# Memory rows copied into v's own tile, sums by four-column products, router inputs turned by PE, and reordered units, in a kernel of chunked attention and top-2 experts

## The chip, the cores and the metric

The kernel runs on one core of a Trainium2 chip. A core has five engines with lists of their own: PE (TensorE, matrix products; its weight loads are shown as PEld), DVE (VectorE), ACT (ScalarE), POOL (GpSimd) and SP (SyncE, which here only issues DMAs). Sixteen DMA engines serve the DMAs of all of them. Each engine works through its list in order, and waits between engines go over semaphores. The metric is the device time of one execution in microseconds (us); lower is better.

## What is computed

Attention over chunks of 32 queries, each with a context of 16 keys to the left, the chunk itself, 8 to the right, and 8 memory keys of its head; then a router that takes the best two of eight experts for each of the 3072 rows.

```python
for c in range(nc):                                   # 24 chunks of 32
    k_full = np.concatenate([mem_k, k[:, :, l_start:r_end]], axis=2)
    v_full = np.concatenate([mem_v, v[:, :, l_start:r_end]], axis=2)
    scores = scale * np.matmul(q_c, k_full.transpose(0, 1, 3, 2))
    a = np.exp(scores - np.max(scores, axis=-1, keepdims=True))
    a = a / (np.sum(a, axis=-1, keepdims=True) + 1e-09)
    out[:, :, c_start:c_end] = np.matmul(a, v_full)
...
logits = x @ w_gate
noisy_logits = logits + np.log1p(np.exp(x @ w_noise)) * noise
top2 = np.argpartition(-noisy_logits, 2, axis=1)[:, :2]
# the softmax of the two gives the weights of relu(x @ w1[e]) @ w2[e]
```

Shapes: q, k and v are 4 x 8 x 768 x 64 in float32 (batch, heads, rows, depth), mem_k and mem_v 4 x 8 x 8 x 64, x is 3072 x 512, there are 8 experts of 512 x 1024 and 1024 x 512.

## The kernel before

**Units and groups.** The attention is cut into 16 units (NPAIR). A group g of four heads has two units, each with half of the 24 chunks. q and k of a group are loaded by POOL into qg and kg (three buffers each), v into one of three tiles vg (load_v, four DMAs, L120). In a tile vg each head has 32 partitions: 28 hold the context rows (two rows side by side), the last four are for memory and are zero in this kernel. For that, each of the three tiles is cleared once, in pieces, by DVE (zero_v, L136), ACT (clear_v, L159) and POOL (L570, L571).

**A unit's steps**, in the main loop from L576. Iteration i works at several units at once: PT_pe(i-1) turns the probabilities on PE, max_dve(i) takes the maximum of the scores (L298), qkT_pe turns q and k of a later head pair (L250), PT_dve(i-1) copies the turned probabilities to SBUF (L317), sub_dve(i) subtracts the maximum on DVE (sd, L303) and takes the exponential on ACT (P, L305). kT_act copies the turned keys in two halves on ACT (kd, L261), PV_pe(i-1) makes the value products, scores_pe(i+1) the next scores, mult_dve(i-1) divides by the sum (rec, L342, and xrow, L343), and xT_pe(i-2) turns the rows for the router (p_x, L354; copied to xt, L356). ps_s and ps_o, the PSUM tiles of scores and values, have one buffer, the turned tiles share a ring of three (tag "tr").

**Keys ahead.** ahead(i) says which head pairs are turned in iteration i: i+2 up to iteration 4, both i+2 and i+3 in iteration 5 (NEAR), and i+3 from then on. The scores of an even unit need the keys of two pairs, its own and the next.

**The memory rows.** mem_v is loaded by SP into mv_nat, cast by POOL (memory_values, L186) into a tile memv with one block of columns a head and four more columns of ones. For each of the three blocks u of a unit, two products with memv of 260 columns (L326) start the accumulation: 256 columns of memory values and four of sums over all keys. The products with vg (L330) add the context's values.

**The router.** The weights (wgn_f) and the noise (nz_all) are loaded by SP in rows of 32 bytes (load_router, load_noise), cast on DVE (L227). begin_route(b), after the units of batch b, makes the logits on PE (L365), and the steps of route(b) are run piece by piece in later iterations by early_steps and late_steps, partly on DVE, ACT and POOL. write_rows (L533) writes the rows x and their gates to DRAM from SP's list. After the loop come the last unit, the last batch's routing, the lists of rows for each pair of experts, and the experts: gathers by POOL (L682), products L746 and L754, and scattered writes (L762).

**What sets the order.** The engines' lists are in the order in which the code is written (the schedule is manual); nothing moves an instruction past another of its engine.

Of the kernel before, what the change touches and what calls it, by code (L numbers as in the profile page):

```python
# [12 lines left out]
F32 = mybir.dt.float32  # L13
# [11 lines left out]
def kernel(  # L25
# [59 lines left out]
    def body():  # L85
# [28 lines left out]
        def load_v(g):  # L114
            vg = groups[g][2]
            for hd in range(2 * GP):
# [6 lines left out]

                first, last = gh == 0, gh == B * H - 1
# [12 lines left out]

        new_group(0)
# [8 lines left out]
        mv_nat = ap_.tile([128, NG, 2, D], F32, name="mv_nat", bufs=1)  # L147
        nc.vector.memset(mv_nat, 0.0)
        for hd in range(2 * GP):
            nc.sync.dma_start(  # L150
                out=mv_nat[QW * hd + WP:QW * hd + QW].rearrange("p g e d -> p g (e d)"),
                in_=bass.AP(mem_v.tensor, mem_v.offset + hd * n_mem * D, [[2 * D, n_mem // 2], [2 * GP * n_mem * D, NG], [1, 2 * D]]))
# [11 lines left out]
        for x in range(3):  # L164
            zero_v(0, x)
        load_v(0)
# [10 lines left out]
        memv = ap_.tile([128, NG, 2, OW], BF16, name="memv", bufs=1)  # L177
        nc.vector.memset(memv, 0.0)
        for hd in range(2 * GP):
            p0 = QW * hd  # L180
            nc.vector.memset(memv[p0:p0 + QW, :, :, MD + hd:MD + hd + 1], 1.0)

        def memory_values(lo, hi):
            for hd in range(2 * GP):
                p0 = QW * hd
                nc.gpsimd.tensor_copy(memv[p0:p0 + QW, lo:hi, :, hd * D:hd * D + D], mv_nat[p0:p0 + QW, lo:hi])  # L186

# [3 lines left out]
        wgn_f = rp.tile([128, KP, 2, E], F32, name="wgn_f")  # L191

        def load_router():
            for x, src in enumerate((moe_w_gate, moe_w_noise)):
                nc.sync.dma_start(out=wgn_f[:, :, x, :], in_=src.rearrange("(kp p) e -> p kp e", p=128))
            load_noise(0)

        nz_all = rp.tile([128, NP, E], F32, name="nz_all")

        def load_noise(b):  # L200
            nc.sync.dma_start(out=nz_all[:, b * BT:(b + 1) * BT, :], in_=moe_noise[b * S:(b + 1) * S].rearrange("(t p) e -> p t e", p=128))

# [20 lines left out]
        def constants():  # L223
# [3 lines left out]
            nc.vector.tensor_copy(wgn, wgn_f.rearrange("p k t e -> p k (t e)"))  # L227
# [5 lines left out]
        def memory_keys():  # L233
# [3 lines left out]
            for hh in range(2):  # L237
                nc.scalar.copy(mkd[64 * hh:64 * hh + 64, :, hh, :], p_m[64 * hh:64 * hh + 64])

# [17 lines left out]
        def kT_act(n):  # L257
# [280 lines left out]
        def begin_route(b):  # L538
# [7 lines left out]
            for x in ((1,), (2, 3))[b] if b < 2 else ():  # L546
                load_noise(x)
# [420 lines left out]
```

## Time and profile before

| | us |
|---|---|
| median of 3 runs | 343.18 |
| lowest and highest of them | 341.76, 344.17 |
| the profiled execution, its own time | 340.9 |
| its span in the trace | 339.2 |
| busy in the span: PE, DVE, ACT, POOL | 295.1, 170.8, 132.5, 137.9 |

Attention and routing take about the first 108 us: the first gather is issued at 107.45 us and the first expert product starts at 112.89 us. In the page's slices each digit is the busy share of one fortieth of the span in tenths; PEclk is the clock granted to PE, DMA the mean busy share of the sixteen DMA engines. A row of a view gives the start and length in us, the line and engine, what is written and read, and in brackets the idle time of the engine ahead of it and what ended it. In a row of groups the numbers behind the first bar are the busy time in all and the mean length in ns; behind the second the idle time ahead of the group.

### The profile page before, as it was taken

What the parts mean: (1) busy time and instruction counts of PE and PEld (TensorE: products, weight loads), DVE (VectorE), ACT (ScalarE), POOL (GpSimd) and SP (SyncE); (2) the same over time, 40 slices, a digit from 0 to 9 for tenths busy, and PEclk for the clock granted to TensorE, in tenths of its full rate; (3) what the DMA queues carried; (4) which work ended last, traced back from release to release, by engine and by line L of the source; (5) the groups of instructions that cost most, each with busy time, mean ns of one, the idle gap of its engine ahead of it and who ended that gap; (6) DMA issues with size and microseconds to landing.
All of it is one profiled execution on the core that took longest, in us unless ns stands there. A gap on an engine that the chain in (4) does not pass through costs nothing.

```text
span 339.2 us, 8160 instructions
## 1 busy us (share of the span) xinstructions
PE 295.1 (87%) x3492; PEld 180.0 (53%) x3492; DVE 170.8 (50%) x341; ACT 132.5 (39%) x232; POOL 137.9 (41%) x181
## 2 busy tenths in 40 slices
PE   1687888898753859999999999999999999999990
PEld 1566676776542645548547545545545545545540
DVE  7788779889686653224224233224413424434430
ACT  7867888795430423343333323223123113103100
POOL 8878885392233686400062043034250132141161
PEclk9999999999985699999999999999999999999997
DMA  7999999999991379970059129518849227221031
GB/s 102 183 180 192 187 164 198 221 104 164 228 276 26 96 111 226 224 130 2 2 84 229 31 60 198 95 56 148 181 107 200 57 80 126 40 93 53 6 130 66
DMA packets 58407, 42.87 MB, mean 126 GB/s; under 512 B 32215, under 2 KB 51799, under 8 KB 58368
## 3 DMA queue, kind: packets, MB, share of 16 engines
q0 software_dynamic: 49808, 38.80, 68.9%
q1 hardware_dynamic: 8272, 3.44, 4.7%
q8 instruction: 29, 0.48, 0.5%
q10 hardware_dynamic: 288, 0.07, 0.1%
q14 instruction: 10, 0.08, 0.1%
HBM read 61.32 MB, written 10.65 MB: 212 GB/s over the span
## 4 chain that ended last, share of the span: by engine, by line
PE 54%; issue 16%; DVE 15%; ACT 6%; POOL 5%; DMA 1%; POOLq 0%; DVEq 0%
PE ps_h L746 23%; PE ps_y L754 19%; POOL out_dram L762 4%; ACT kd L261 3%; DVE vg L136 2%; DVE mx L298 2%; DVE sd L303 2%; PE p_t L691 2%; DVE xrow L343 2%; PE ps_o L330 2%; PE ps_o L326 2%; ACT xt L356 2%; ACT P L305 1%; ACT qT L253 1%; PE ps_s L285 1%
## 5 line engine op out<-in xcount | busy, mean ns | idle before, releaser
L746 PE MATMUL ps_h<-xTb,w1t 128*128 128x512 bf16 (+3 forms) x608 | 106.6, 325 | 2.0 <-DVE xTb L692 2.0
L754 PE MATMUL ps_y<-w2t,ht 128*128 128x512 bf16 x448 | 102.0, 379 | 0.0
L746 PEld LDWEIGHTS <-w1t 128*128 128x128 bf16 x864 | 64.1, 97 | 45.2 <-DVE xTb L692 1.6
L762 POOL DMA_INDIRECT out_dram<-acc,sidx x28 | 27.9, 995 | 139.2 <-DVE acc L761 135.0
L734 DVE TENSOR_SCALAR ht<-ps_h 128x416 bf16<-128x416 f32 (+2 forms) x64 | 39.9, 625 | 72.8 <-PE ps_h L746 72.8
L732 ACT ACTIVATE ht<-ps_h 128x416 bf16<-128x416 f32 (+2 forms) x72 | 37.9, 526 | 76.7 <-PE ps_h L746 72.4
L754 PEld LDWEIGHTS <-ht 128*128 128x128 bf16 x448 | 41.9, 98 | 46.6
L758 ACT ACTIVATE acc<-ps_y,meta 128x512 f32<-128x512 f32 x28 | 19.2, 687 | 69.3 <-PE ps_y L754 56.5
L746 PE MATMUL ps_h<-xTs,w1t 128*128 128x32 bf16 x256 | 45.4, 177 | 0.2 <-DVE xTs L707 0.2
L761 DVE SCALAR_TENSOR_TENSOR acc<-ps_y,meta,acc 128x512 f32<-128x512 f32 x28 | 21.0, 751 | 37.0 <-PE ps_y L754 37.0
L682 POOL DMA_INDIRECT xl<-x_rows,gidx x28 | 29.7, 1061 | 15.4 <-issue 6.1
L120 POOL DMA_DIRECT2D vg<-in_v_dram x34 | 25.3, 753 | 8.2 <-PE ps_s L290 3.4
L692 DVE COPY xTb<-p_t 128x512 bf16<-128x512 bf16 x28 | 11.7, 422 | 29.0 <-PE p_t L691 29.0
L261 ACT COPY kd<-p_t 64x768 bf16<-64x768 bf16 x32 | 25.2, 786 | 1.0 <-PE p_t L250 0.7
L250 PE MATMUL p_t<-identb,qg 128*64 128x128 bf16 x192 | 10.3, 245 | 8.2 <-DMA qg<-in_q_dram 6.3
L305 ACT ACTIVATE P<-sd 128x768 bf16<-128x768 f32 x16 | 13.5, 844 | 9.5 <-DVE sd L303 9.5
L356 ACT COPY xt<-p_x 128x768 bf16<-128x768 bf16 x16 | 12.8, 798 | 8.0 <-PE p_x L354 7.7
L343 DVE TENSOR_TENSOR xrow<-ps_o,rec 128x768 bf16<-128x768 f32 x16 | 15.3, 958 | 0.6
L326 PE MATMUL ps_o<-memv,PT 128*128 128x260 bf16 x96 | 13.7, 279 | 2.0 <-DVE PT L317 2.0
L298 DVE TENSOR_REDUCE mx<-ps_s 128x12 f32<-128x768 f32 x16 | 15.1, 941 | 0.6 <-PE ps_s L285 0.6
L303 DVE TENSOR_TENSOR sd<-ps_s,mx 128x768 f32<-128x768 f32 x16 | 15.2, 947 | 0.0
L253 ACT COPY qT<-p_t 128x768 bf16<-128x768 bf16 x16 | 12.8, 800 | 5.0 <-PE p_t L250 4.7
(146 smaller groups left out, 305.6 us busy)
## 6 DMA issues: line engine op xcount, KB each, us to landing
w1t<-in_moe_w_dram POOLq DMA_DIRECT2D x8, 1024.0 KB
w2t<-in_moe_w_dram POOLq DMA_DIRECT2D x8, 1024.0 KB
vg<-in_v_dram POOLq DMA_DIRECT2D x30, 168.0 KB
qg<-in_q_dram POOLq DMA_DIRECT2D x7, 384.0 KB
kg<-in_k_dram POOLq DMA_DIRECT2D x7, 384.0 KB
x_rows<-xrow SPq DMA_DIRECT2D x3, 792.0 KB
x_rows<-xrow SPq DMA_DIRECT2D x2, 384.0 KB
xl<-x_rows,gidx POOLq DMA_INDIRECT x28
```

The source lines that it names most:

```text
L120: nc.gpsimd.dma_start(out=vg[p0 + j:p0 + j + nj, c:c + n, hd, :, :].rearrange("p c e d -> p c (e d)"), in_=bass.AP(v.tensor, v.offset + (g ...
L261: nc.scalar.copy(st[n]["kT"][hs, hh, :].rearrange("d (p j) -> d p j", j=SJ), st[n]["p_k"][hs].rearrange("d j p -> d p j"))
L298: nc.vector.tensor_reduce(out=mx, in_=st[n]["ps"], axis=AX, op=Alu.max)
L303: nc.vector.tensor_tensor(out=sd, in0=st[n]["ps"], in1=bc4(st[n]["mx"], CTX), op=Alu.subtract)
L343: nc.vector.tensor_tensor(out=xr.rearrange("p u (h d) -> p u h d", d=D), in0=po[:, :, :MD].rearrange("p u (h d) -> p u h d", d=D), in1=rec ...
L682: nc.gpsimd.indirect_dma_start(out=xl, out_offset=None, in_=xd, in_offset=bass.IndirectOffsetOnAxis(ap=gidx[:, p:p + 1], axis=0), bounds_c ...
L732: nc.scalar.activation(out=dst, in_=src, func=Act.Relu)
L734: nc.vector.tensor_scalar(out=dst, in0=src, scalar1=0.0, scalar2=None, op0=Alu.max)
L746: nc.tensor.matmul(out=ps_h[:, o:o + w], lhsT=w1t[:, kp, f * 128:(f + 1) * 128], rhs=rhs(kp), start=(kp == 0 and i == 0), stop=(kp == KP - ...
L754: nc.tensor.matmul(out=ps_y, lhsT=ht[:, f, j * CAP:(j + 1) * CAP], rhs=w2t[:, f, :], start=(f == 0), stop=(f == FB - 1))
L761: nc.vector.scalar_tensor_tensor(out=a, in0=ps_y, scalar=gate, in1=a, op0=Alu.mult, op1=Alu.add)
L762: nc.gpsimd.indirect_dma_start(out=out_part[p], out_offset=bass.IndirectOffsetOnAxis(ap=sidx[:, p:p + 1], axis=0), in_=a, in_offset=None, ...
```

## The change

The memory rows go into the four spare partitions of each head in vg. POOL loads them once, cast to bfloat16, into a small tile mv of 16 partitions, and load_v has, ahead of each head's v load, one more DMA on SP's list: it copies four partitions of mv into vg, the same row for each of the 24 chunks. memv, mv_nat, memory_values and their clearing go. The 260-column products become products with headb, a constant of four columns (one a head), which give only the sums; the products with vg give the memory's values with the others.

Pieces of the second and third vg tile that DVE and POOL cleared are now cleared by POOL as 32-bit words (wipe_v).

The noise and the router weights are loaded at the start as rows of 4 KB into 32 partitions (rowsT), three DMAs on SP. After unit 3, router_turn turns them with eight products on PE and copies them into nz_all and wgn with three copies on ACT. The later noise loads and the cast go.

The units' order: ahead(i) is always i+2. From unit 1 on the first half of the key copies goes ahead of the exponential on ACT, the second stays behind it. begin_route goes behind the value products and the next scores. In the last iteration late_steps comes ahead of the value products, and mult of unit 14 goes behind PT of unit 15; xT of unit 14 goes behind the last value products.

```diff
+                nc.sync.dma_start(out=vg[p0 + WP:p0 + QW, :, hd, :, :].rearrange("p c e d -> p c (e d)"),
+                                  in_=mv[MP * hd:MP * hd + MP, g:g + 1, :].to_broadcast([MP, ncnk, 2 * D]))
...
+        def wipe_v(x, lo, hi):
+            nc.gpsimd.memset(vbufs[x][:, lo:hi].bitcast(I32), 0)
+
+        NW = 2 * KP
+        rowsT = ap_.tile([NP + NW, 128, E], F32, name="rowsT", bufs=1)
+        nc.sync.dma_start(out=rowsT[:NP], in_=moe_noise.rearrange("(t p) e -> t p e", p=128))
+        for x, src in enumerate((moe_w_gate, moe_w_noise)):
+            nc.sync.dma_start(out=rowsT[NP + KP * x:NP + KP * (x + 1)], in_=src.rearrange("(kp p) e -> kp p e", p=128))
...
-        mv_nat = ap_.tile([128, NG, 2, D], F32, name="mv_nat", bufs=1)
-        nc.vector.memset(mv_nat, 0.0)
...
+        MP = QW - WP
+        mv = ap_.tile([2 * GP * MP, NG, 2 * D], BF16, name="mv", bufs=1)
...
+        nc.gpsimd.dma_start(out=mv, in_=bass.AP(mem_v.tensor, mem_v.offset, [[2 * D, 2 * GP * MP], [2 * GP * n_mem * D, NG], [1, 2 * D]]))
         load_v(0)
...
-        memv = ap_.tile([128, NG, 2, OW], BF16, name="memv", bufs=1)
-        nc.vector.memset(memv, 0.0)
+        headb = const.tile([128, 2 * GP], BF16, name="headb")
+        nc.vector.memset(headb, 0.0)
         for hd in range(2 * GP):
...
+            nc.vector.memset(headb[QW * hd:QW * hd + QW, hd:hd + 1], 1.0)
...
+        def router_turn():
+            p_n = psT.tile([128, E, NP + NW], F32, name="p_n", tag="tr")
+            for e in range(E):
+                nc.tensor.transpose(out=p_n[:, e, :], in_=rowsT[:, :, e], identity=ident)
+            nc.scalar.copy(nz_all, p_n[:, :, :NP].rearrange("p e t -> p t e"))
+            for x in range(2):
+                nc.scalar.copy(wgn[:, :, E * x:E * x + E], p_n[:, :, NP + KP * x:NP + KP * (x + 1)].rearrange("p e k -> p k e"))
...
-        def kT_act(n):
+        def kT_act(n, which=(0, 1)):
...
-                    nc.tensor.matmul(out=po[:, u, :OW], lhsT=PT[:, 2 * u + e, :], rhs=memv[:, g, e, :], start=(e == 0), stop=False, skip_group_check=True)
+                    nc.tensor.matmul(out=po[:, u, MD:OW], lhsT=PT[:, 2 * u + e, :], rhs=headb, start=(e == 0), stop=(e == 1), skip_group_check=True)
...
-        memory_values(0, 2)
-        nc.gpsimd.memset(vbufs[1][:, 12:15], 0.0)
-        nc.gpsimd.memset(vbufs[1][:, 21:24], 0.0)
+        wipe_v(1, 12, 15)
+        wipe_v(1, 21, 24)
+        wipe_v(1, 6, 12)
         def ahead(i):
-            return [i + 2] if i < NEAR else [n for n in (i + 2, i + 3) if n < NPAIR and (i == NEAR or n > i + 2)]
+            return [i + 2] if i + 2 < NPAIR else []
...
-            if fresh:
-                begin_route((i - 3) // HP)
             early_steps()
             if i >= 1:
                 PT_dve(i - 1)
+            if i >= 1:
+                for n in ahead(i):
+                    kT_act(n, (0,))
             sub_dve(i)
             if i == 0:
-                zero_v(1, 1)
                 load_v(1)
...
+            if i == NPAIR - 1:
+                late_steps()
             for n in ahead(i):
-                kT_act(n)
+                kT_act(n, (1,) if i >= 1 else (0, 1))
...
                 scores_pe(i + 1)
+            if fresh:
+                begin_route((i - 3) // HP)
             if i < NPAIR - 1:
                 late_steps()
-            if i in (2, 3, 4):
-                zero_v(2, i - 2)
-            if i >= 1:
+            if 1 <= i < NPAIR - 1:
                 mult_dve(i - 1)
...
+            if i == 1:
+                wipe_v(2, 0, 12)
...
             if i == 3:
-                zero_v(2, 3, nc.gpsimd)
+                wipe_v(2, 12, 24)
                 ramps()
-                load_router()
+                router_turn()
...
         PT_pe(n)
         PT_dve(n)
-        xT_pe(n - 1)
-        late_steps()
+        mult_dve(n - 1)
+        write_rows(B, B - 1, 0, UB, 0, XC)
         PV_pe(n)
         mult_dve(n)
         write_rows(B + 1, B - 1, UB, BT, 0, XC)
+        xT_pe(n - 1)
         early_steps()
         xT_pe(n)
```

26 lines of the change are left out of this document (1 added, 25 removed).

## The prediction

> **What bounds the kernel now.** I read the slices of the page first, then the chain that ended last, then the rows of each engine in order of time, then the DMA view by windows.
>
> ```profile
> PE   1687888898753859999999999999999999999990
> ...
> PEclk9999999999985699999999999999999999999997
> DMA  7999999999991379970059129518849227221031
> ```
>
> A slice is 8.5 us. From slice 15 on PE is full and DMA often idle: the expert products, which the change doesn't touch, set the time there. What the change can move lies in slices 0 to 12, attention and routing, where PE is at 7 to 8 tenths and, what is easily passed over, **DMA at nine tenths or more in every slice from 1 to 11**. The chain of waits goes there from engine to engine:
>
> ```profile
> 13.38 1.34 DVE vg L136
> 14.72 0.82 DVE mx L298
> ...
> 31.29 0.68 ACT kd L261
> 31.99 0.80 ACT kd L261
> 33.40 0.96 DVE mx L298
> ```
>
> So three things are late by turns: memsets on DVE (units 0 to 4), key copies on ACT (odd units), and later DVE's own list, with gaps in which DVE waits for PE:
>
> ```profile
> L342 DVE RECIPROCAL rec<-ps_o 128x12 f32<-128x12 f32 x11 | 2.5, 229 | 6.3 <-PE ps_o L330 6.1
> ```
>
> This row is of the window 46 to 98 us: 6.1 us of waiting for the value products before the reciprocal.
>
> **Part 1, the four-column sums.** One unit's PE rows (start, length):
>
> ```profile
> 35.13 0.84 PE L326 MATMUL ps_o<-memv,PT 128*128 128x260 bf16 x6
> 35.91 0.85 PE L330 MATMUL ps_o<-vg,PT 128*32 128x256 bf16 x24
> 36.69 0.31 PE L275 MATMUL ps_s<-mkd,qT 128*128 128x16 bf16 x6
> 36.92 0.51 PE L285 MATMUL ps_s<-kd,qT 128*32 128x112 bf16 x23
> ```
>
> From start to start the six 260-column products take 0.78 us. Six products of 16 columns with the same full weight load (L275) take 0.23; four columns can't be dearer, and the weight load stays. So 0.55 us a unit, 8.8 over 16, of which only that part counts where DVE waits for the value products.
>
> **Part 2, work taken from DVE and POOL.**
>
> ```profile
> L136 DVE MEMSET vg<- 128x1536 uint32 x8 | 10.7, 1338 | 2.3 <-issue 2.3
> ```
>
> Four of the eight L136 memsets leave DVE (5.4 us), and with them the clearing of memv and mv_nat; five far smaller ones come for headb. On POOL the wipes write 32-bit words, 9,216 a partition (2 x 768, 1536, 2 x 3072); at the rate of the row below, 0.87 ns an element, that is 8.0 us. They replace this memset, two of half its size (5.3 us together) and eight casts, so POOL has about as much to do as now, and one more DMA to issue (mv). Its loads are issued well ahead of their turn on the engines (part 5), which hides this; without that cover a load would come up to 8.0 us later.
>
> ```profile
> 34.68 2.66 POOL L136 MEMSET vg<- 128x3072 bf16 x1
> ```
>
> **Part 3, reordering.** Odd units' scores wait for the keys of unit i+2 behind the exponential (the two kd rows above). With one half moved ahead of it, one half, 0.8 us, goes. At unit 5 the before kernel turns two units at once:
>
> ```profile
> 41.63 3.21 ACT L261 COPY kd<-p_t 64x768 bf16<-64x768 bf16 x4
> ```
>
> Half of this, 1.6 us, goes. The price: from unit 7 on odd units wait again for their own keys, which the before kernel had a unit ahead. begin_route goes behind the value products and the scores, so its 24 products no longer stand before them at units 6, 10 and 14:
>
> ```profile
> 85.20 0.74 PE ps_l L365 x24
> ```
>
> **Part 4, router_turn** adds eight 32-bit transposes and three ACT copies after unit 3. Four such took 0.63 us:
>
> ```profile
> 8.63 0.63 PE L236 MATMUL p_m<-ident,mk_nat 32*128 32x32 f32 x4
> ```
>
> So 1.3 us of PE; its PSUM buffer also holds up the next key transposes. I count 1.3 on the path, nothing if PE waits for v then anyway.
>
> **Part 5, the copies on SP.** Per group four DMAs of 4 x 24 rows of 256 bytes, 384 packets; 32 DMAs in all. SP is in order: behind a copy that waits for a buffer stand later copies and the x_rows writes. The waits are for the same value products that POOL's v loads wait for already, and the writes are not needed before the gathers, so I give that nothing; if a write were held up, it would have until the gathers. But the packets use engines that are full:
>
> ```profile
> DMA packets 3315, 0.90 MB, mean 180 GB/s; under 512 B 3009, under 2 KB 3314, under 8 KB 3314
> ...
> DMA packets 879, 0.60 MB, mean 200 GB/s; under 512 B 165, under 2 KB 878, under 8 KB 878
> ...
> DMA packets 3598, 0.83 MB, mean 166 GB/s; under 512 B 3596, under 2 KB 3596, under 8 KB 3596
> ...
> DMA packets 4960, 1.11 MB, mean 186 GB/s; under 512 B 4193, under 2 KB 4960, under 8 KB 4960
> ...
> q1 hardware_dynamic: 2016, 0.06, 43.2%
> ```
>
> These are the windows 34 to 39, 39 to 42, 44 to 49 and 10 to 16 us. Small packets are v, larger ones q and k. In 34 to 39 some 3,009 small ones pass, about a group of v (28 x 24 x 4 = 2,688), then q and k follow: so group 2's v is there at about 39.0. Its user, and the maximum of unit 6 behind it:
>
> ```profile
> 42.28 0.85 PE L330 MATMUL ps_o<-vg,PT 128*32 128x256 bf16 x24
> ...
> 44.76 0.94 DVE L298 TENSOR_REDUCE mx<-ps_s 128x12 f32<-128x768 f32 x1
> ```
>
> Only 3.3 us of slack. The loads run back to back, so a faster attention stage can't have them earlier. By then the copies of groups 0 to 4, 5 x 384 = 1,920 packets, are mixed in. Spread over all engines at v's own rate (3,596 packets in 5 us) they cost 2.7 us; at that of the 2,016 packets of 32 bytes, which left the total at 186 GB/s, nothing. I take 1.3: v of group 2 at 40.3. [...]
>
> **The sum.** First stretch, to the maximum of unit 6: without v the engines gain 0.5 (an estimate between nothing and the 1.34 of the memset that ends at 14.72, when unit 0's maximum starts), 2 x 0.8 (units 1, 3), 2 x 0.55 (units 2, 4), 1.6 (unit 5), and lose 1.3: 3.5, maximum at 41.3. With v at 40.3 and the 2.48 us from L330 to the maximum it comes at 42.8: **-2.0** (ends -3.3 and -0.6). Second stretch, units 6 to 15: of the 6.1 us of waits four are long; 4 x 0.55, and 0.7 at three of them for the routing products, is 4.3. But the transposes of unit i+2 stay ahead of the value products and wait for ACT, and odd units wait for keys (partly covered by DVE's routing steps): **-1.8** (ends -4.3, all of it, and +1, none of it and a quarter us more at each of units 7, 9, 11 and 13). Tail:
>
> ```profile
> 93.75 0.51 PE p_x L354 x6
> ```
>
> xT of unit 14 leaves PE's list before the last value products, the routing steps fill DVE's wait before, and mult of unit 14 goes behind PT of 15: **-0.5** (ends -1, twice the transposes, and +0.5, PT of 15 ahead of that mult and nothing gained). Sum -4.3 us. The profiled execution took 340.9 us, of which 339.2 are the span; it would come to 334.9 and 336.6. The median of the runs shown is 343.18, 2.3 above it, so I predict 338.9.
>
> **The rivals.** Two maxima of DVE, of units 8 and 15, and the sizes of the loads:
>
> ```profile
> 54.81 0.95 DVE L298 TENSOR_REDUCE mx<-ps_s 128x12 f32<-128x768 f32 x1
> ...
> 88.62 0.95 DVE L298 TENSOR_REDUCE mx<-ps_s 128x12 f32<-128x768 f32 x1
> ...
> vg<-in_v_dram POOLq DMA_DIRECT2D x30, 168.0 KB
> qg<-in_q_dram POOLq DMA_DIRECT2D x7, 384.0 KB
> ```
>
> *Slower: the copies pile on a few DMA engines.* A copy writes four partitions. If it runs on four of the 16 engines, always the same, these get 1,920 / 4 = 480 packets more by the time of group 3's v. At v's price, 16 x 5 us / 3,596 = 22 ns on one engine, that is 10.7 us. Behind group 2's v at 39.0 come the 768 KB of q and k of a group and the 672 KB of group 3's v, 3.9 and 4.1 us at the 200 and 166 GB/s of the rows: 47.0, and in this case 57.7. The maximum of unit 8 comes some 2.5 us after the product that uses it, as for unit 6 above: 60.2 in place of 54.8. The seven units from there take 33.8 now and 32.0 with the gain of the second stretch; the tail gains its 0.5. So 343.18 + (60.2 + 32.0 - 88.6) - 0.5 = 346.3. From some 16 ns a packet on it is slower than before. For it: DMA at nine tenths, and no slack to take up a delay; against it: the 32-byte packets that cost nothing, and that v's packets read 512 bytes from DRAM for their 256 and a copy reads half of that from SBUF. [...] No view of this profile names an engine.
>
> *Little change: half of that price.* At 11 ns the 480 packets are 5.3 us: unit 8's maximum at 47.0 + 5.3 + 2.5 = 54.8, where it is now, so that all of the first stretch is lost; and if the odd units' key waits take 0.6 of the later gain, 343.18 + (54.8 + 32.6 - 88.6) - 0.5 = 341.5. For it: bytes in place of packets set the price; against: as above.
>
> *More: the copies are free*, and the waits for the value products go nearly whole: -3.3, -3.5 and -0.7, which is 335.7. For it: the 32-byte packets; against: the transposes and keys that still stand in the same lists.
>
> **How the numbers follow.** Forecast 0.45, free copies 0.13, little change 0.25, slower 0.17. About 1% (3.4 us) is what a measurement of this kernel tells from no change. Faster by more: 0.37 of the forecast and all of the free case, 0.50. Slower by more than 1%, 346.6 and up: the piling case above v's price, or with PE waits that it adds elsewhere, 0.12. Within: 0.38. The range goes from a little below the free case to the piling one, 335 to 347, and leaves out what goes beyond either.
>
> **What would show it.** Right: L326 at about 0.23 us for six; no L136 memset on DVE after 14 us; unit 6's maximum at 42 to 43.5 and unit 15's at 84 to 86; PE waiting before the value products of unit 4 for v. Piling: v loads of one group that land far apart, unit 8's maximum after 56. Wrong would be a maximum of unit 6 as late as now, a wait on the copies themselves in units 0 to 2, or a start of the expert products that moves by another amount than unit 15's maximum.

## The result, and the profile after

The changed kernel takes 359.36 us, the median of four runs (358.79 to 359.57), against 342.75 us for the kernel before on the same chip: 1.051 times as long (95% interval 1.047 to 1.055), some 17 us more. The forecast was 338.9, in a range of 335 to 347. The profiled execution has a span of 357.9 us. A few executions were slower at a lower mean clock (one of e5's four took 352.16 us at 0.950, the other three 345.56 to 348.48 at 0.958 to 0.968); the times and ratios below leave those out.

The page's slices come first; a slice is now 8.9 us. The last line is that of the kernel before, for comparison.

```profile
PE   2718858578776358899999999999999999999990
...
PEclk9976788698888559999999999999999999999997
DMA  7999998999999424998006904913949624421031
GB/s 109 172 167 160 162 131 88 145 209 103 184 192 206 149 80 74 214 192 202 2 3 99 222 4 91 217 27 93 204 114 161 116 97 76 70 99 51 3 126 63
...
GB/s 102 183 180 192 187 164 198 221 104 164 228 276 26 96 111 226 224 130 2 2 84 229 31 60 198 95 56 148 181 107 200 57 80 126 40 93 53 6 130 66
```

The full stretch of PE begins two slices later than before. In slice 2 (counted from 0) PE stands nearly still, its clock is below full in most slices up to 14, and the DMA engines, at eight or nine tenths as before, move less: 131 and 88 GB/s in slices 5 and 6, where it was 164 and 198. The chain of waits says what holds the attention up (start, length, what):

```profile
15.30 0.82 SPq L124
...
17.52 10.46 DMA vg<-mv
...
28.23 1.48 PE ps_o L327 x24
...
32.84 0.24 PE ps_o L323 x6
33.07 0.82 PE ps_o L327 x24
...
36.44 15.87 DMA vg<-in_v_dram
52.30 0.28 issue
52.58 17.42 DMA vg<-in_v_dram
70.01 0.28 issue
70.29 0.75 POOL vg L120
71.06 0.53 POOL oh L427
...
76.01 16.46 DMA vg<-in_v_dram
```

First the copies of the memory rows themselves: issued on SP from 15.3 us, the last of group 0 lands 10.5 us after its issue. Then three v loads of 16 to 17 us each. Before, this part of the chain went from engine to engine. POOL now often issues a load only when an earlier one has landed, 12.3 us of waits by the page's group below (first row; the second is the kernel before), and its routing step oh (L427 in the chain) stands behind these issues.

```profile
L120 POOL DMA_DIRECT2D vg<-in_v_dram x34 | 25.4, 752 | 26.8 <-DMA vg<-in_v_dram 12.3
...
L120 POOL DMA_DIRECT2D vg<-in_v_dram x34 | 25.3, 753 | 8.2 <-PE ps_s L290 3.4
```

DVE's rows show the first of the stalls and the maxima that answer to those of the prediction (units 2, 6, 8 and 15):

```profile
29.77 0.23 DVE L339 RECIPROCAL rec<-ps_o 128x12 f32<-128x12 f32 x1 [9.77 <-PE ps_o L327]
30.04 0.96 DVE L340 TENSOR_TENSOR xrow<-ps_o,rec 128x768 bf16<-128x768 f32 x1
30.91 0.95 DVE L295 TENSOR_REDUCE mx<-ps_s 128x12 f32<-128x768 f32 x1
...
54.68 0.95 DVE L295 TENSOR_REDUCE mx<-ps_s 128x12 f32<-128x768 f32 x1
...
68.31 0.95 DVE L295 TENSOR_REDUCE mx<-ps_s 128x12 f32<-128x768 f32 x1
...
107.03 0.94 DVE L295 TENSOR_REDUCE mx<-ps_s 128x12 f32<-128x768 f32 x1
```

Unit 6's maximum is 9.9 us later than before, unit 8's 13.5, unit 15's 18.4; the first expert product starts at 131.68, 18.8 later. So all of the loss lies ahead of the experts. Three rows of the lists of waits name the cause of the first stall, and what it holds up (what waited, for what, us in total, times, longest). SP can't issue the first copies before 15.3 us, since mv's own load has to land; PE then waits 9.0 us for the copies; and POOL waits 6.9 us for the value products that free a tile, so that the v loads of group 2 are issued from 34.18 us on, where it was 26.68 before:

```profile
SPq L124 <- DMA mv<-in_mem_v_dram: 13.3, 1, 13.3
...
PE ps_o L327 <- DMA vg<-mv: 9.0, 1, 9.0
...
POOL vg L120 <- PE ps_o L327: 6.9, 1, 6.9
```

The windows of 10 us show the clock beside the stall (engines' busy times, then the granted clock, DMA share and GB/s; the second pair is the kernel before):

```profile
10.00:20.00 10.00, 7.23 (x140) 5.82 (x140) 6.16 (x8) 8.76 (x12) 6.42 (x8) 1.00 1.81 168
20.00:30.00 10.00, 1.77 (x32) 1.29 (x33) 0.23 (x1) 1.38 (x2) 7.25 (x8) 0.62 1.78 170
...
10.00:20.00 10.00, 7.15 (x138) 5.88 (x136) 8.70 (x14) 8.49 (x12) 7.59 (x11) 1.00 1.71 189
20.00:30.00 10.00, 8.43 (x198) 6.44 (x197) 8.65 (x14) 7.00 (x10) 8.11 (x12) 1.00 1.45 175
```

After the nine idle microseconds the same 24 products take 1.48 us (28.23 in the chain), and 0.82 five microseconds later. In the traces of these two kernels the granted clock is either full or half (1.00 or 0.50); up to unit 15's maximum it is half for 36.9 us in the changed kernel, and never in the kernel before. Stalls and lower clock go together here; no run separates them.

The trace also has the time of each of the 16 completions that a load posts. This is worked out from them, and is no view of the page: the last v load of group 2, in us.

```
kernel                                   issued  first  12th   13th   16th
before                                    28.93   37.5   38.8   38.9   39.2
changed                                   36.44   41.8   44.0   49.6   52.3
e1, no copies                             30.58   39.0   40.7   40.9   42.1
e2, copies to a spare tile, 4 partitions  33.19   41.0   43.8   49.5   50.4
e3, copies to a spare tile, 16 partitions 31.31   40.5   43.0   43.2   43.5
e7, changed, tiles realigned              35.28   38.7   40.8   44.4   46.0
e11b, the same, packets of 1 KB           31.88   38.1   39.5   42.6   45.0
e8, copies issued by POOL                 46.23   48.5   49.6   49.6   50.2
```

Twelve completions come together and four come late, the last by 8.3 us in the changed kernel. In the trace a copy into four partitions has four records as its data land, and one about a microsecond after its issue (the first copy of the changed kernel, issued at 15.30 us, has one at 16.58 and four from 22.64 to 23.45); a copy into 16 has 16. Four late ones of 16 fit the piling on four engines that the prediction had as its slower rival. But no view here names an engine: that the four late completions stand for four engines, and the same four each time, was not shown.

### The profile page after: what moved, and what is told of

Its sections match the earlier page's. It is cut to its first block, busy times and chain, and to the rows that moved or that the text cites. A ratio compares the mean times of both kernels' runs of the same rounds, so it can differ in the third digit from the quotient of the medians.

```text
span 357.9 us, 8223 instructions
## 1 busy us (share of the span) xinstructions
PE 297.3 (83%) x3500; PEld 183.8 (51%) x3500; DVE 164.7 (46%) x335; ACT 132.2 (37%) x235; POOL 136.5 (38%) x176
## 4 chain that ended last, share of the span: by engine, by line
PE 64%; DMA 19%; DVE 5%; POOL 4%; issue 3%; ACT 2%; SPq 1%; POOLq 0%; DVEq 0%
PE ps_h L742 29%; PE ps_y L750 25%; DMA vg<-in_v_dram 14%; DMA vg<-mv 3%; PE ps_o L327 2%; DMA kg<-in_k_dram 2%; PE p_t L687 2%; POOL out_dram L758 1%; PE ps_s L769 1%; POOL vg L120 1%; PE p_t L247 1%; DMA xl<-x_rows,gidx 1%; PE ps_s L282 1%; DVE xrow L340 1%; ACT kd L258 1%
## 5 line engine op out<-in xcount | busy, mean ns | idle before, releaser
L120 POOL DMA_DIRECT2D vg<-in_v_dram x34 | 25.4, 752 | 26.8 <-DMA vg<-in_v_dram 12.3
L327 PE MATMUL ps_o<-vg,PT 128*32 128x256 bf16 x384 | 17.4, 327 | 16.8 <-DMA vg<-mv 9.0
L327 PEld LDWEIGHTS <-PT 128*32 128x32 bf16 x384 | 10.9, 110 | 18.2 <-issue 9.1
L247 PE MATMUL p_t<-identb,qg 128*64 128x128 bf16 x192 | 11.3, 273 | 7.3 <-DMA qg<-in_q_dram 6.5
L282 PE MATMUL ps_s<-kd,qT 128*32 128x112 bf16 (+2 forms) x384 | 12.0, 254 | 5.3 <-ACT kd L258 5.3
L340 DVE TENSOR_TENSOR xrow<-ps_o,rec 128x768 bf16<-128x768 f32 x16 | 15.3, 957 | 0.6
## 6 DMA issues: line engine op xcount, KB each, us to landing
kg<-in_k_dram POOLq DMA_DIRECT2D x7, 384.0 KB, 15.3
```

What stands on the lines that cost most here:

```text
L120: nc.gpsimd.dma_start(out=vg[p0 + j:p0 + j + nj, c:c + n, hd, :, :].rearrange("p c e d -> p c (e d)"), in_=bass.AP(v.tensor, v.offset + (g ...
L327: nc.tensor.matmul(out=po[32 * r:32 * r + 32, u, :MD], lhsT=PT[:, 2 * u + e, 32 * r:32 * r + 32], rhs=vg[:, CB * half + x, :, e, :], start ...
L340: nc.vector.tensor_tensor(out=xr.rearrange("p u (h d) -> p u h d", d=D), in0=po[:, :, :MD].rearrange("p u (h d) -> p u h d", d=D), in1=rec ...
```

## Experiments

Each run stands beside the kernel before on the same chip; ratios are to that, with 95% intervals. Starts of the maxima of five units, and of the first expert product, from the timelines of all profiles, in us (one profiled execution each; that of the kernel before, 340.9 us, was faster than its other runs, 341.76 to 344.17, so a difference of a microsecond or two is not safe):

```
kernel               unit 2  unit 6  unit 8  unit 11 unit 15  experts  ratio
before                23.25   44.76   54.81   69.99   88.62   112.89
changed               30.91   54.68   68.31   84.76  107.03   131.68   1.051
e1_nocopy             23.41   44.70   57.42   75.67   95.02   119.44   1.013
e2_spare4             22.74   53.36   63.66   79.24  102.31   127.10   1.039
e3_spare16            23.68   46.69   60.29   77.33   96.96   121.74   1.026
e4_reorder            23.75   42.00   51.51   71.07   91.50   116.49   1.001
e5_before_pad32       23.43   45.77   57.55   74.02   92.66   117.03   1.014
e6_nocopy_pad         21.94   42.88   53.95   69.34   89.00   112.79   0.996
e7_after_pad          29.50   48.38   62.52   76.83   96.79   121.39   1.028
e8_poolcopy_pad       27.92   52.90   69.66   88.64  112.15   135.94   1.062
e9b_near              22.32   45.02   55.25   72.40   92.02   116.37   1.002
e10b_reorder_near     23.51   43.49   53.86   70.14   90.01   114.36   1.001
e11b_big              24.01   47.50   58.19   75.04   94.54   121.03   1.019
e12b_big_near         25.86   49.30   59.49   76.50   96.55   122.04   1.012
e13_first             22.92   43.55   54.04   70.07   88.70   113.03   0.996
e14_first4            22.31   42.75   53.39   70.27   89.68   114.07   1.005
e15_route_early       21.84   42.77   53.17   69.41   88.76   114.07   1.001
e16_four              22.37   43.31   54.20   69.94   88.78   111.50   0.992
e17_four_turn         21.91   45.28   57.03   72.87   91.75   115.25   1.000
e18_first_four        22.14   43.07   54.79   71.05   88.93   113.92   0.993
```

### The copies, and where their packets go

**e1_nocopy** leaves the copies out.

```diff
-                nc.sync.dma_start(out=vg[p0 + WP:p0 + QW, :, hd, :, :].rearrange("p c e d -> p c (e d)"),
-                                  in_=mv[MP * hd:MP * hd + MP, g:g + 1, :].to_broadcast([MP, ncnk, 2 * D]))
```

> The 32 copies of the memory rows are left out, so the values of the memory rows don't enter the sums; everything else is as in the changed kernel. Theory A, the copies cost it: at least 16 us come back, about 339 (336 to 343), unit 15's maximum near 86, and a group's v lands again in about 12 us rather than 16. Rival B, the order of the work (score, route and tail moved): the time stays above 350, because the copies go but the order stays. Rival C, both: 345 to 350.

347.68 us, ratio 1.013 (1.005 to 1.022). That is C: about 13 of the 17 us go (0.0375 of 343), and a kernel is left that is still slower than before. Something else costs too.

**e2_spare4 and e3_spare16** send the copies to a tile that nothing reads; POOL clears a column of mv behind each group's first load (0.14 us each), so that the copies aren't issued ahead of their group's loads. They still come some microseconds later than the real ones did: for group 1 from 23.9 us in e2 and 22.0 in e3, where it was 18.4.

```diff
+                if hd == 0 and g > 0:
+                    nc.gpsimd.memset(mv[:, g].bitcast(I32), 0)
-                nc.sync.dma_start(out=vg[...], in_=...)
+                # e2: four partitions, 24 packets on each
+                nc.sync.dma_start(out=spare[4 * hd:4 * hd + 4], in_=mv[4 * hd:4 * hd + 4, g:g + 1, :].to_broadcast([4, ncnk, 2 * D]))
+                # e3: sixteen partitions, six packets on each
+                nc.sync.dma_start(out=spare[:, 6 * hd:6 * hd + 6], in_=mv[:, g:g + 1, :].to_broadcast([16, 6, 2 * D]))
```

> The copies leave the value tile and go to a spare tile that nothing reads, as many and as large as before (four partitions each, 24 packets of 256 bytes on each); the memory values don't enter the sums. Nothing can wait for a copy's end except SP. Theory A1, the packets pile on four DMA engines and make the loads late: 352 to 360, near the changed kernel. Rival A2, the value products wait for the copies themselves: near the kernel without copies, 336 to 343.

> The same copies to the spare tile, same number, bytes and packets, but each over 16 partitions with six packets on each. Theory A1, piling on four engines: back to within 4 us of the kernel without copies, at least 8 us faster than the spare tile by four partitions. Rival A3, the packets cost what they cost wherever they go: the same as the spare tile by four partitions, within 3 us.

e2: 355.37 us, 1.039 (1.031 to 1.046). e3: 350.55, 1.026 (1.018 to 1.034). The median time of a v load from issue to landing, between 15 and 70 us, for e1, e2 and e3 in turn:

```profile
vg<-in_v_dram POOLq DMA_DIRECT2D x24, 168.0 KB, 9.0
```

```profile
vg<-in_v_dram POOLq DMA_DIRECT2D x20, 168.0 KB, 13.7
```

```profile
vg<-in_v_dram POOLq DMA_DIRECT2D x24, 168.0 KB, 10.4
```

No engine but SP waits for these copies, and still four partitions cost 4.2 us more than sixteen (1.2% of 343), with the same packets and bytes. So it counts over how many partitions a copy goes, as with piling, and that is not all: copies over sixteen partitions cost 1.3% too (e3 against e1, seven short memsets on POOL included). The intervals overlap a little for both steps, but they share the runs of the kernel before; the runs of the three kernels themselves, on one chip, don't overlap (344.65 to 347.87, 349.59 to 352.35, 354.07 to 356.06). The step from e2 to the changed kernel is another 1.2%; it goes with the wait for the copies themselves (unit 2's maximum: 22.7 in e2, 30.9 in the changed kernel), but that wait wasn't taken out alone. e3 missed its own mark of 8 us. The rival "free when nothing waits for them" is out.

**e8_poolcopy_pad** issues the copies from POOL's list in place of SP's.

> As the changed kernel with the tile of 224 bytes, and the 32 copies issued by POOL in place of SP, same shapes. POOL issues four more per group at some 0.75 us each. Theory A1, the same four engines: if POOL's copies are dealt out over other engines each time, the time falls by 5 or more against SP's copies with the tile, to 341 to 346, less what POOL's 24 us of issues hold up. Rival A3, the packets cost the same wherever they go: no better than SP's copies, or worse by POOL's issues.

365.64 us, 1.062 (1.054 to 1.071), the slowest of all, where A1 had a fall of 5 us or more; A3 had "worse by POOL's issues". The four late completions are gone (49.6 and 50.2 in the table), but the time went up. POOL's 32 issues take 21.8 us, its loads and its routing steps stand in the same list, and the last load of group 2 is issued 11 us later than in e7. This run can't price the piling.

**e11b_big and e12b_big_near** lay the value tile out head by head and hold the memory rows four times over (mv4), so that a copy is six packets of 1 KB a partition; e12b also turns keys three units ahead.

```diff
+        vbufs = [ap_.tile([128, 2 * GP, ncnk, 2, D], BF16, name=f"vg{i}", bufs=1) for i in range(NVB)]
...
+                nc.sync.dma_start(out=vg[p0 + WP:p0 + QW, hd].rearrange("p (o r) e d -> p o (r e d)", r=4),
+                                  in_=mv4[MP * hd:MP * hd + MP, g].rearrange("p (o r) x -> p o (r x)", o=1).to_broadcast([MP, ncnk // 4, 8 * D]))
```

> The changed kernel, aligned by the tile of 224 bytes, with the value tile laid out head by head and the memory rows held four times over, so that each copy is six packets of 1 KB on each of its four partitions in place of 24 of 256 bytes; same bytes, same four partitions. Theory A1 by packets (each packet takes its turn with one of the loads on its engine): the copies cost a quarter of the 11 us, ratio 0.998 to 1.008, unit 2's maximum at 22 to 25. Rival, bytes on four engines: as the aligned changed kernel, 1.024 to 1.034, unit 2's maximum near 29.

> The same with q and k turned three units ahead from unit 5 on as before; all of the reference is computed. If theory E and the theory of packets both hold: 0.985 to 0.997, faster than both kernels. If only the packets: as the one without this, 0.998 to 1.008.

349.13 us, 1.019 (1.014 to 1.024), and 347.38, 1.012 (1.007 to 1.017). The price falls by a third against e7, between the two bands, and the four late completions stay (39.5 and 45.0). So a quarter of the packets doesn't make it a quarter of the price. But the edit changes more than the packets: mv4's loads stand earlier in POOL's list, so that the copies of group 0 are issued from 10.84 us in place of 15.02, and in the compiled programs mv4 starts on a multiple of 256 bytes where mv in e7 is 128 past one. What the bytes, the packets and these two have of it stays open. That both theories hold, by which e12b would have beaten both kernels, is out.

### The addresses

The change takes a tile of 256 bytes a partition (wgn_f) out of an early pool and puts in headb, which takes 32. The tiles behind them move: by the compiled program vg starts at byte 63232 of a partition before, which is 247 x 256, and 224 lower at 63008 after, 32 past a multiple of 256; the tiles of q and k, too, start on a multiple of 256 before and 32 past one after. v's packets are 256 bytes, q's and k's 768.

**e5_before_pad32** puts 32 unused bytes ahead of everything in the kernel before; **e6_nocopy_pad** and **e7_after_pad** put 224 into e1 and into the changed kernel.

```diff
+        const.tile([128, 16], BF16, name="pad")     # e5; e6 and e7: [128, 112]
```

> The kernel before with an unused tile of 32 bytes per partition in front of everything else; nothing else is changed. All tiles of the attention stage move from addresses that are multiples of 256 bytes to 32 bytes past one, as they lie in the changed kernel. Theory D, address: each packet of 256 bytes then straddles a boundary and takes longer; the loads pass at some 170 GB/s in place of 185 to 190 between 15 and 40 us, and the time goes up by 3 to 8 us (345 to 350). Rival: addresses don't matter, 341 to 343 and the same rate.

> The changed kernel without the copies (the values of the memory rows don't enter the sums), and with an unused tile of 224 bytes per partition, which puts the value, query and key tiles back to the addresses modulo 256 that they have in the kernel before. Theory D: back to 336 to 341, 6 or more below the same kernel without the tile (347.7). Rival, the other edits (router rows turned by PE, four-column sums, one more load on POOL) cost the 6 us: 346 to 349.

> The changed kernel whole, with the same unused tile of 224 bytes. Theory D and the copies add up: 348 to 353 (359.4 less some 7, the copies still there). If the address were all of it: 341 or below. If the copies were all of it: 357 to 360.

e5: 347.21 us, 1.014 (1.005 to 1.022; only three runs, and the medians alone, against 344.23, give 0.9%). e6: 343.14, 0.996 (0.992 to 0.999). e7: 353.97, 1.028 (1.022 to 1.035). e5 is as expected (between 15 and 40 us 173 GB/s against 185); e6 and e7 fall somewhat less far than they should have, e6 to a time between its two bands. The queue rows between 15 and 70 us (packets, MB, their time as a share of 16 engines), for the kernel before, then e5:

```profile
DMA packets 29296, 10.28 MB, mean 187 GB/s; under 512 B 22372, under 2 KB 29284, under 8 KB 29284
...
q0 software_dynamic: 26891, 9.24, 143.4%
```

```profile
DMA packets 27295, 9.88 MB, mean 180 GB/s; under 512 B 20372, under 2 KB 27284, under 8 KB 27284
...
q0 software_dynamic: 25186, 8.88, 169.5%
```

A packet takes 1.434 x 16 x 55 us / 26,891 = 46.9 ns before and 59.2 ns in e5, and the rate falls from 187 to 180 GB/s, from an unused tile alone. In three kernels the shift costs 1.3 to 2.2% by the ratios (e5 against before, e1 against e6, changed against e7). Nothing but the places of the tiles in SBUF moved in e5; why a packet takes longer there no view shows.

### What the rest is worth

**e4_reorder** is the kernel before with the new order, the split key copies, the wipes and the tail; **e10b_reorder_near** the same with keys turned three units ahead from unit 5 on, **e9b_near** e6 with that, **e15_route_early** e6 with begin_route ahead of the value products again.

```diff
         def ahead(i):                                  # e9b, e10b: as before
-            return [i + 2] if i + 2 < NPAIR else []
+            return [i + 2] if i < NEAR else [n for n in (i + 2, i + 3) if n < NPAIR and (i == NEAR or n > i + 2)]
```

```diff
             if i + 1 < NPAIR:
                 scores_pe(i + 1)
-            if fresh:                                  # e15: back ahead of early_steps()
-                begin_route((i - 3) // HP)
```

> The kernel before with the reordered units, the key copy in two halves, the wipes on POOL and the new tail alone; memory sums, casts and router loads as before. By the prediction's terms without the four-column sums (first stretch 0.5 + 1.6 + 1.6, second stretch 3 x 0.7, tail 0.5): 4 to 6 us faster than before, 337 to 339. Rival B, the order costs it: 350 or more. Little change, 341 to 345, if POOL's wipes beside its casts hold up the loads.

> The changed kernel without the copies (the values of the memory rows don't enter the sums), aligned by the tile of 224 bytes, and with one thing of the order put back: from unit 5 on q and k are turned three units ahead again, as in the kernel before. Theory E, the keys: in the aligned kernel without copies the steps from odd units to even ones (7, 9, 11, 13) are some 0.8 us longer than in the kernel before, since the scores of the next pair wait for keys turned in the same unit; with the order put back 2.5 to 4 us go, ratio 0.984 to 0.989 against 0.996. Rival, PE's waits for instructions or the clock take it: no change, 0.993 to 0.999.

> The kernel before with the reordered units, the key copy in two halves, the wipes on POOL and the new tail, but q and k turned three units ahead from unit 5 on as before; memory sums and router loads as before. Theory E: 0.985 to 0.993 of the time before (the reordered kernel without this had 1.001). Rival: as that one, 0.997 to 1.005.

> The aligned changed kernel without the copies (the values of the memory rows don't enter the sums), with the 24 routing products put back ahead of the value products and nothing else. Theory F, if it is the routing products: 1.5 to 3 us faster than with them behind, 0.987 to 0.992. The prediction had them cost 0.7 us at three units there: 0.999 to 1.003. Rival G: 0.994 to 0.998.

Ratios: e4 1.001 (0.997 to 1.006), e9b 1.002 (0.998 to 1.005), e10b 1.001 (0.998 to 1.005), e15 1.001 (0.998 to 1.005). Each says no change against the kernel before, and e9b and e15 are, if anything, some 0.5% slower than e6 (the intervals overlap). For e15 that is the band that goes with the prediction's own price of the routing products, 0.7 us at three units; theory F falls there. In e6 PE waited for keys (first row, 40 to 100 us: total, times, longest), and with the keys turned earlier (e9b, second fence) less than half is left; but then it waits for the routing step oh on POOL, and for nothing that the profile shows ("issue").

```profile
PE ps_s L281 <- ACT kd L257: 4.5, 4, 1.4
```

```profile
PE ps_r L433 <- POOL oh L426: 2.9, 2, 1.9
...
PE p_x L350 <- issue: 2.0, 1, 2.0
PE ps_s L281 <- ACT kd L257: 1.9, 1, 1.9
```

Theory E falls: the wait for keys was there, of the size supposed, and another took its place.

The diffs of these five are in part against the changed kernel. **e13_first** keeps the change's order up to unit 5 and in the tail only; **e16_four** is the kernel before with the four-column sums and without memory values; **e18_first_four** has both; **e14_first4** has both and the turned router rows; **e17_four_turn** is e16 with the turned rows.

```diff
-            if i >= 1:
+            if 1 <= i <= NEAR:                          # e13, e14, e18: the split only up to unit 5
                 for n in ahead(i):
                     kT_act(n, (0,))
```

```diff
-                    nc.tensor.matmul(out=po[:, u, :OW], lhsT=PT[:, 2 * u + e, :], rhs=memv[:, g, e, :], start=(e == 0), stop=False, skip_group_check=True)
+                    nc.tensor.matmul(out=po[:, u, MD:OW], lhsT=PT[:, 2 * u + e, :], rhs=headb, start=(e == 0), stop=(e == 1), skip_group_check=True)   # e14, e16 to e18
...
-                load_router()
+                router_turn()                           # e14, e17
```

> The kernel before with the change's order only up to unit 5 and in the tail (half of the key copy moved ahead, clearing on POOL, one unit turned at a time until unit 5, the new tail); from unit 6 on the order of the kernel before, the routing products ahead of the value products among it; all of the reference is computed. Theory F, the new order of the routing products and key copies gives the gain of the first stretch back from unit 6 on: the gain of some 2 us at unit 6's maximum stays, unit 15's maximum 86 to 87, ratio 0.990 to 0.995. Rival G, the second stretch takes up any lead since it is held by a chain from PE to ACT and DVE and by PE's waits for instructions that the order doesn't set: 0.998 to 1.003.

> The same order with four-column sums and router rows turned by PE, without the copies (the values of the memory rows don't enter the sums), aligned. By the prediction's term the four-column sums give 0.55 us at each of four or more units: 0.984 to 0.990 by theory F. Rival G: 0.993 to 0.999 as with the changed order (0.996).

> The kernel before with the four-column sums in place of the 260-column products, and without memory values, their casts and clearing; order, router loads and addresses modulo 256 as before. The prediction's terms for this alone (0.55 at units 2 and 4 and at four of the later units, and the clearing of two tiles off DVE's list): 2.5 to 4 us faster, 0.988 to 0.993. Rival G, the products lie where PE waits for others anyway: 0.997 to 1.001.

> The kernel before with four-column sums (memory values left out) and with noise and router weights as long rows turned by PE, order as before, addresses aligned. The same without the turned rows had 0.992. The prediction's term for the turned rows, 1.3 us on the path: 0.995 to 0.998. Rival H, turning the rows by PE costs most of what the four-column sums bring and more (the kernel with the early order, four-column sums and turned rows had 1.005): 1.002 or more. If they cost nothing: 0.990 to 0.994.

> The order changed up to unit 5 and in the tail as in e13, with four-column sums (memory values left out), and router loads as before: e13 with the sums, or e14 without the turned rows and the early load of the memory rows. If the gains of e13 (0.9955) and of the sums (0.9924) add: 0.986 to 0.990. If both only shorten the same waits, or rival G holds for the two together: 0.991 to 0.998.

e13 0.996 (0.991 to 1.000), e14 1.005 (1.001 to 1.009), e16 0.992 (0.988 to 0.997), e17 1.000 (0.997 to 1.004), e18 0.993 (0.989 to 0.996). The four-column sums, with the casts, loads and memsets that go with them, bring 0.8%, 2.6 us, about what was forecast for them alone; but in e16's profile the lead of 1.5 us at unit 6 is gone at unit 15, and 1.4 us show only at the first expert product. Order and sums don't add (e18). e13 and e17 fall between their bands, and e14 is slower than all of its. The turned rows take 0.8% (e17 against e16) to 1.2% (e14 against e18; e14 also loads the memory rows). In the profiles of e16 and e17 the step from unit 4 to unit 5 is 4.9 and 6.6 us; e17 first, then e16:

```profile
32.07 0.96 DVE L289 TENSOR_REDUCE mx<-ps_s 128x12 f32<-128x768 f32 x1 [0.30 <-PE ps_s L276]
...
38.66 0.95 DVE L289 TENSOR_REDUCE mx<-ps_s 128x12 f32<-128x768 f32 x1
```

```profile
32.52 0.96 DVE L286 TENSOR_REDUCE mx<-ps_s 128x12 f32<-128x768 f32 x1 [0.30 <-PE ps_s L273]
...
37.41 0.95 DVE L286 TENSOR_REDUCE mx<-ps_s 128x12 f32<-128x768 f32 x1
```

The eight turns are 1.09 us of that. In e17 PE's clock was at half between 33 and 38 us (0.50), in e16 at full (1.00), and in e14, which has the turns too, at full. One trace can't say whether the turns bring the clock down, but every run has its mean granted clock, and over the runs behind the ratios these fall into groups: 0.962 to 0.968 with the 260-column products (the kernel before on each chip, e4, e10b, e13), 0.951 with the four-column sums (e16, e18), 0.934 to 0.948 with the turned rows as well (e6, e9b, e14, e15, e17). With a clock that is full or half, as in the traces before and after the change, 0.951 in place of 0.965 is some 10 us more at half clock (2 x 0.014 x 343, an estimate). So both edits go with a lower clock; how much of their time that is, and whether PE's lighter load brings it, no run here separates.

No complete kernel here is more than 0.5% faster than the one before; e13 is the only one whose interval lies below the kernel before, and it ends at no change.

## Why the prediction was wrong

The forecast had -4.3 us; 1.051 of 343 is +17.4. In its own terms:

| term | forecast, us | shown, us | from |
|---|---|---|---|
| copies on SP | +1.3 | +11.2 | e7 less e6: 0.0326 of 343 |
| addresses | none | +7.6 | changed less e7: 0.0222 of 343 |
| everything else | -5.6 | -1.4 | e6: 0.9959 |
| sum | -4.3 | +17.4 | |

The split depends on the order: with the copies taken out first they are 12.9 us (changed less e1) and the addresses 5.9 (e1 less e6). By the intervals each of these differences is good to 2 to 4 us.

**The step that failed first is Part 5**: "Spread over all engines at v's own rate (3,596 packets in 5 us) they cost 2.7 us; at that of the 2,016 packets of 32 bytes, which left the total at 186 GB/s, nothing. I take 1.3: v of group 2 at 40.3." The loads weren't delayed evenly: of the 16 completions of group 2's last v load twelve are there at 44.0 us and the last at 52.3, or at 40.8 and 46.0 with the tiles realigned (e7). The slower rival came nearest, also in size, with 10.7 us for packets piled on four engines (by the same completions the last v load of group 3 lands at 59.5 in e7, 11.7 later than before, part of it from a late start), and got a chance of 0.17. No run shows that a copy runs on four engines, always the same; what the runs show is four late completions of 16, and 4.2 us between copies into four partitions and into sixteen (e2 less e3). Against it stood two rows that say nothing of which engine a packet runs on: packets of 32 bytes that left the total at 186 GB/s, and the bytes that a copy reads. A mean share over 16 engines can't speak for or against four of them being late. The rival's time, 346.3, was still too short, since it left the gains and the addresses as forecast. The copies' bare price at the front was missing as well: those of group 0 are issued from 15.3 us, land up to 10.5 us later, and their user waits 9.0 us; the v loads that should have been "issued well ahead of their turn" (Part 2) then start late too. The prediction named a wait on the copies in units 0 to 2 as a sign that it is wrong, and had no term for it.

**The addresses were in no step.** The diff takes a tile out of one pool and puts one into another, and nothing in the two kernels' code says where the tiles then lie.

**The rest**, seen in e6, where copies and addresses are out. The first stretch gave part of its gain: unit 6's maximum at 42.88 is 1.9 us earlier than before, where the prediction's own terms without the copies give -3.3. That this is near the -2.0 forecast for the whole change is luck, since that figure had a cost of the copies in it; the changed kernel has +9.9. The second stretch went the other way: from unit 6 to unit 15 it takes 46.1 us against 43.9 before, +2.3 where -1.8 was forecast, beyond the end of +1. The waits for value products that were to go did go down, but waits for keys (named, priced at a quarter of a microsecond each, up to 1.4) and others came in their place, and putting the keys or the routing products back brought no time. The tail's -0.5 isn't shown: from unit 15's maximum to the first expert product it is 23.8 us in e6 and 24.3 before, but other kernels with the new tail take up to 26.5, and e16 and e17, with the old one, 22.7 and 23.5. Why the second stretch gives the lead back whichever order it has isn't settled: e13, with the order of the kernel before from unit 6 on, loses a lead of 1.2 us there as well, in its one profile; over its runs it is some 0.5% faster than before. The clock isn't the reason in the profiles of e6 and e13: between units 6 and 15 it is at full in both.

**Smaller points.** Part 1: six four-column products take 0.24 us (the chain's row at 32.84), 0.23 forecast, and their worth, with what goes with them, is 2.6 us in e16. Part 2: the last memset of vg on DVE starts at 9.9 us, as forecast; the wipes on POOL weren't tried by themselves. Part 4: the turns are 1.1 us of PE for 1.3 forecast, and cost 2.7 to 4.2 us of time by the ratios (the upper figure has the early load of the memory rows in it). That SP's order costs nothing wasn't tried by itself. PE did wait for v ahead of unit 4's value products, and unit 8's maximum came after 56, both signs named in advance.

## What to carry to other kernels

Before adding small copies beside full-width loads, ask over how many partitions one copy goes; here copies that write four partitions left four of the 16 completions of the v loads beside them late, the last by 8.3 us, and cost 4.2 us more than copies over sixteen (e2 less e3), though the mean DMA share hardly moved. After any change of tile sizes compare the start addresses of the tiles that DMAs fill, and try an unused tile in front if they moved: here 32 bytes past a multiple of 256 cost 1.3 to 2.2% by the ratios. And a lead won early in a stage counts only if the units behind it keep it; in the profiles here leads of 1 to 3 us at unit 6 were gone at unit 15.

## What was not expected of the hardware

32 bytes of shift cost about 1% with nothing else changed (e5: 0.5 to 2.2% by the interval): 46.9 ns a packet against 59.2.

PE can stand still for 2 us while nothing that the profile shows is awaited. In e4, whose lead of 3.3 us at unit 8 was gone one unit later, between two halves of one turn:

```profile
53.76 0.48 PE L357 MATMUL p_x<-identb,xrow 128*128 128x128 bf16 x3 [2.04 <-issue]
54.03 0.85 PE L315 MATMUL p_p<-identb,P 128*128 128x128 bf16 x6
```

One packet of the queue for instructions, 16 KB, is under way from 51.52 to 52.50 us, beside full loads; PE stands still for 1.3 us longer, and the trace doesn't say whose instructions it brings, so a late fetch of PE's program is no more than a guess. The six p_p products that follow take 0.85 us, against 0.50 one unit later: the granted clock is at half from 52.98 us for 6.8 us. So the stop of 2 us costs more than itself; unit 9's maximum comes 9.7 us after unit 8's, where it was 4.8 before.

From the first expert product to the end, code that no experiment touched, the profiles of these kernels took between 225 and 230 us. So a difference of a microsecond or two between two profiled executions there says nothing.
